# Keys and queries turned in token pairs, growth products written over alpha, and a new order of steps, in a gated-attention and hard-swish kernel

## The chip, the core and the metric

The kernel runs on one core of one Trainium2 chip. The core has five engines with queues of their own: TensorE (PE in the profile; its weight loads are PEld), VectorE (DVE), ScalarE (ACT), GpSimd (POOL), and SyncE (SP), which issues the DMAs. The metric is the device time of one execution in microseconds (us), lower is better. The kernel before takes 533.33 us, the median of three runs from 532.68 to 533.54 us.

## The reference, cut to what matters

```python
def _attn_ref(q, k, v, alpha):            # (4, 8, 768, 48) each
    state = np.zeros((B, H, D, D))
    for t in range(S):
        state = alpha[:, :, t, :, None] * state + np.einsum('bhd,bhe->bhde', k[:, :, t], v[:, :, t])
        y[:, :, t] = np.einsum('bhd,bhde->bhe', q[:, :, t], state)

def _moe_ref(x, w_in, w_out):             # x: attention's output as (3072, 384); d_ff = 2048
    h = x @ w_in
    g = h * np.clip(h + 3.0, 0.0, 6.0) / 6.0
    return g @ w_out
```

A linear attention with a decay for every channel and token is followed by a two-layer network with a hard-swish between the layers. The two weight matrices arrive as 64-bit floats and are rounded to 32 bits on the core.

## The kernel before, in words

**Attention.** The 4 x 768 tokens are cut into 24 chunks of 128. For a chunk `j`, alpha, keys and queries are turned so that a partition holds a channel (two heads of 64 rows each at a time, four such pairs of heads side by side) and the 128 tokens lie along the free dimension. A reversed scan over alpha gives the products R towards the end of the chunk (`decay`, step `r`, L309) and a reciprocal of its four first values goes into the tile `ini` (L313). A forward scan over alpha that starts from `ini` gives the growth products P (`growth`, step `p`, L320). The keys are multiplied by R and the queries by P (`scaled`, steps `k` and `q`, L332). Then come scores (`sc`, L346), mask (`m`, L356), the placing of queries and state beside them (`qa` L366, `sv` L419), the state's update (`u` L430, `sm` L438 and L440, `st` L409) and the attention's output, which is written turned (`ya` and `yb`, L456; `cy`, L465). P and the two `ini` tiles hold 4 x 129 values in a partition: each group of 128 tokens has one value ahead of it, where alpha is 0 so that the scan starts anew.

**How a chunk is turned.** Chunks 0 to 5 are turned by TensorE (steps `ta`, `tk`, `tq`, L282). From chunk 6 (`FIRST = 6`) VectorE turns blocks of 32 x 32 (`by_blocks`, L286). The load (L262) puts token 4u+v of a chunk into block v, row u, so one turn of 128 x 512 reads runs of 32 words and writes each turned row with a step of 4 words:

```python
nc.vector.transpose(out=to.rearrange("r p (u v) -> r p v u", v=V),
                    in_=quads[name, j % NQ][:, :, :, 0:BLK])
```

For keys and queries it writes straight into `Ks[j % 2]` or `Qs[j % 2]`, and `scaled` then multiplies in place. From chunk 8, the scaled keys are turned back by token in another way: a turn on VectorE that writes whole runs (`kt`, L391), a DMA out (`kw`) and a DMA back (`kr`).

**The two layers.** Two chunks make a pair `g` of 256 tokens. Pairs 0 and 1 go through the first layer plainly (steps `f`, `fa`, `fb`, L479 and L490; their gate is `fr` on ScalarE, L495, and `fg` on VectorE, L499), and pair 0 through the second (`b`, L517). Pairs 2 to 11 take the first layer as 20 products of sums of x and sums of weights (`M`, L603), with the sums of weights built once (`y`, L540 to L544), sums of x for every pair (`xc`), copies out of PSUM (`n`, L609), sums of products (`o`), gate (`e` L495, `h` L499). Pairs 1 to 11 take the second layer as 7 products of sums (`P`, L706; sums `s`, L650 and L667; `K`, `G` and `O` bring results out). One `M` step is 8 entries on PE, one `P` step 16.

**The order.** All steps stand in one string of 1798 words, such as `tq.9` or `M.3.10`, under a manual schedule. Each engine runs its own part of that string strictly in order, and waits where data or a buffer is not ready. The last numbers of a word name a PSUM bank: four banks (`t0` to `t3`) serve the attention, four (`m0` to `m3`) the layers. `z` steps are idle matmuls on TensorE that compute nothing. The weights' way is load (`w`), low half (`d1`, L186), magnitude (`d2`, L196), high bits (`d3`, L207 to L210) and addition (`d4`, L217 on GpSimd). In L210 the 64-bit words are worked on in place, so one input and the output step by 2 words.

Of the kernel before, what the change touches and what calls it, by code (L numbers as in the profile page):

```python
# [8 lines left out]
FP = mybir.dt.float32  # L9
# [8 lines left out]
def kernel(  # L18
# [255 lines left out]
    def transposed(name, j, i=None):  # L274
        if j >= FIRST:
            t = (K_t if name == "k" else Q_t)[j] = (Ks if name == "k" else Qs)[j % 2]
            by_blocks(t, name, j)
            return
        t = bank("t" + name, j, i)
        src = ring[name, j % NR]  # L280
        for p in range(NP):
            nc.tensor.transpose(  # L282
                t[:, p], src[:, 2 * p : 2 * p + 2].rearrange("s h d -> s (h d)"), ident)

    def by_blocks(to, name, j):
        nc.vector.transpose(out=to.rearrange("r p (u v) -> r p v u", v=V),  # L286
                            in_=quads[name, j % NQ][:, :, :, 0:BLK])

# [5 lines left out]
    def without_first(t):  # L294
        return t[:, 0 : NP * W].rearrange("r (p w) -> r p w", w=W)[:, :, 1:W]
# [8 lines left out]
    def decay(j):  # L304

        n = NP * W
        ax, ic = aX[j % 2], ini[j % 2]
# [5 lines left out]
        nc.vector.reciprocal(out=ic.rearrange("r (p w) -> r p w", w=W)[:, :, 0:1],  # L313
                             in_=R_t[j][:, :, 0:1])

    def growth(j):

        n = NP * W
        P_t[j] = Ps
        nc.vector.tensor_tensor_scan(  # L320
            out=P_t[j], data0=aX[j % 2][:, 0:n], data1=ini[j % 2], initial=0.0,
            op0=ALU.mult, op1=ALU.add)

    def scaled(name, j):

        if j < FIRST:
# [5 lines left out]
        nc.vector.tensor_tensor(out=t, in0=src, in1=by, op=ALU.mult)  # L332
        (K_t if name == "k" else Q_t)[j] = t
# [423 lines left out]
    with tc.manual_schedule():  # L757
# [18 lines left out]
               p.5 fg.1.3 d2.12 k.5 fg.1.0 d3.12 d4.10 fr.1.6.1 sm.4.1 tq.5.1 sv.4.1 lk.6 w.13  # L776
               fr.1.2.0 d1.11 f.1.4.2 d2.11 d4.12 fg.1.6 q.5 d3.11 p.6 d2.13 la.7 fr.1.4.1 fg.1.4
               f.1.5.0 lv.5.0 qa.4.1 fg.1.2 kb.5.3 fr.1.5.1 w.15 d4.11 d2.15 ca.7 ya.4.1 qa.5.1 tk.6
               yb.4 sc.5.2.0 b.1.0.2 lk.7 k.6 d3.13 d3.15 st.5 ck.5 fa.4.3 m.5 b.1.1 lq.6 w.14 tq.6
               fb.4 fg.1.5 d1.13 d1.15 d4.15 q.6 b.0.0.1 d2.14 fr.0.4.0 d3.14 y.5 d4.13 cy.4 fg.0.4  # L780
               d1.14 d4.14 x.0 y.1 y.10 b.0.1 y.0 y.2 u.5.2 P.1.0.0 K.1.0 qa.5.0 sv.5.0 qa.6.1
               P.1.1.3 b.0.2 b.1.2 kb.6.0 ya.5.3 y.6 s.1.0.0 sm.5.0 sv.5.1 G.1.0.0 tk.7 s.1.1.1
               s.1.2.3 x.1 yb.5 cy.5 b.1.3 sc.6.1.2 lv.6.2 ck.6 u.6.3.0 s.1.3.2 x.2 P.1.2 b.0.3
               K.1.1 y.7 s.1.4 s.1.5 y.11 y.3 r.7 xc.2.1 x.3 y.4 y.8 xc.2.3 k.7 xc.2.0 xc.2.4 y.9
               y.12 y.16 y.13 y.15 P.1.3.3 K.1.2 P.1.4 bo.1 P.1.5 xc.2.5 G.1.1.1 P.1.6 y.14 y.17
               la.8 xc.2.2 xc.2.6 y.19 G.1.3.3 so.1 y.20 G.1.2.2 y.18 M.2.0.2 bo.0 y.21 M.2.15.3
               y.23 sm.6.0 n.2.0.8 z.1.3 M.2.1 M.2.16 xc.2.8 n.2.1.9 xc.2.7 M.2.2 kb.7.3 p.7 lk.8
               O.1.2 lq.7 xc.2.10 sm.6.1 n.2.2.10 ca.8 m.6 M.2.7.0 lq.8 n.2.7.11 M.2.3 M.2.4 M.2.8
               xc.2.9 lv.7.0 r.8 n.2.4.12 tk.8 ck.7 lv.12.1 k.8 M.2.18.1 sv.6.1 o.2.0.0 st.7 M.2.5
               tq.7 kt.8 kw.8 n.2.5.13 M.2.9 q.7 o.2.1.0 sv.6.0 lq.9 o.2.4.0 u.7.1.3 sc.7.1.3 sm.7.0  # L790
               sv.7.0 O.1.3 M.2.10 ya.6.2 yb.6 e.2.1.1 la.9 h.2.1 e.2.0.0 y.22 lv.8.2 p.8 n.2.10.14
               qa.7.0 M.2.11 sv.7.1 M.2.6.2 n.2.18.10 M.2.19 h.2.0 n.2.11.15 qa.7.1 m.7 O.1.1 M.2.12
               cy.6 o.2.6.0 o.2.5.0 ya.7.1 yb.7 n.2.12.12 kr.8 xc.3.2 y.24 M.2.13 lv.9.0 o.2.3.0
               n.2.13.12 cy.7 tq.8 lq.10 sm.7.1 o.2.3.1 M.2.17 o.2.2.0 e.2.3.0 M.2.14 o.2.2.1 xc.3.1
               xc.3.3 la.10 e.2.2.1 P.2.0.1 xc.3.4 xc.3.5 lk.10 xc.3.6 M.3.0.2 q.8 u.8.1.0 lk.9
               sc.8.2.3 n.3.0.12 M.3.1 h.2.2 e.2.5.1 h.2.3 xc.3.0 xc.3.7 o.2.6.1 e.2.6.0 M.3.7.0
               n.3.1.9 o.2.7.0 o.2.7.1 K.2.0.3 h.2.6 M.3.2 P.2.1 qa.8.0 n.3.7.13 e.2.4.0 n.3.2.10
               xc.3.10 xc.3.8 st.8 h.2.5 ca.9 M.3.3 O.1.0 qa.8.1 h.2.4 r.9 s.2.0.14 G.2.0.1 e.2.7.0
# [24 lines left out]
               lq.13 s.4.2.9 P.4.1 h.4.7 xc.5.8 G.4.0.3 s.4.1.12 p.13 M.5.2 tq.13 n.5.2.15 P.4.3.3
               k.13 M.5.3 M.5.4 lq.14 s.4.3.10 K.4.2 sm.12.0 kt.13 n.5.7.8 sm.12.1 O.3.2 s.4.5
# [116 lines left out]
```

## Time and profile before

| | us |
|---|---:|
| median of three runs (532.68 to 533.54) | 533.33 |
| the profiled execution's own time | 533.63 |
| its span, first to last instruction | 531.8 |
| PE busy | 524.3 |
| PEld busy | 494.0 |
| DVE busy | 475.6 |
| ACT busy | 261.4 |
| POOL busy | 50.3 |
| first `M` step starts on PE | 125.65 |
| granted TensorE clock | 1.0 in every slice |

The profiled execution took 533.63 us, of which 531.8 lie between the first and the last instruction and 1.8 around them. It is 0.3 us above the median. PE's records are pipelined and overlap, so a stop of less than about 0.1 us does not show as idle time; it shows only in the distance between the starts of two steps. In the chain that ended last, PE has 85% of the span, VectorE 7% and ScalarE 4%; the `P` products alone have 36% and the `M` products 31%.

### The profile page before, as it was taken

To read this page: it belongs to the slowest core of one execution; us is meant where nothing else is said; L and a number is where in the kernel's file an instruction comes from. 1 tells how busy PE (TensorE), PEld (TensorE's weight loads), DVE (VectorE), ACT (ScalarE), POOL (GpSimd) and SP (SyncE) were. 2 spreads that over 40 slices of the span, in tenths; PEclk is the share of its full clock that TensorE was granted. 3 is DMA by queue.
4 is the path that set the end of the run, shared out by engine and by line. 5 is a ranking of instruction groups with operands and counts; after the bars stand their busy time and mean duration, and the time that the engine had idled before them with its cause. 6 is when DMAs were issued, how large, how long until landed. Compare 5 with 4: busy or idle time off the path is not lost.

```text
span 531.8 us, 15076 instructions
## 1 busy us (share of the span) xinstructions
PE 524.3 (99%) x6290; PEld 494.0 (93%) x6290; DVE 475.6 (89%) x839; ACT 261.4 (49%) x513; POOL 50.3 (9%) x71
## 2 busy tenths in 40 slices
PE   8999999999999999999999999999999999999997
PEld 5798886789999999999999999999999999999997
DVE  7999999999999999999999999998999999486471
ACT  4888875212664453542673554544454454443330
POOL 5333353100000100000000000000000000000000
PEclk9999999999999999999999999999999999999999
DMA  9999867005363253453463553443531532010000
GB/s 177 246 241 251 247 153 177 2 2 133 74 150 84 64 118 77 115 123 89 95 156 85 120 136 91 96 107 69 145 78 20 129 98 48 1 33 7 9 17 30
DMA packets 124100, 54.40 MB, mean 102 GB/s; under 512 B 83328, under 2 KB 116864, under 8 KB 124032
## 3 DMA queue, kind: packets, MB, share of 16 engines
q1 hardware_dynamic: 124032, 53.44, 42.2%
q8 instruction: 49, 0.80, 0.7%
q14 instruction: 19, 0.16, 0.1%
HBM read 44.50 MB, written 8.91 MB: 100 GB/s over the span
## 4 chain that ended last, share of the span: by engine, by line
PE 85%; DVE 7%; ACT 4%; DMA 1%; issue 1%; SPq 1%; POOL 0%; DVEq 0%; ACTq 0%
PE m_ps L706 36%; PE m_ps L603 31%; PE m_ps L479 4%; PE m_ps L517 4%; PE t_ps L456 4%; PE t_ps L346 2%; PE t_ps L430 2%; DMA rings<-in_q_dram 1%; DVE A L356 1%; ACT A L366 1%; DVE g_sb L540 1%; ACT r L495 1%; ACT raw L186 1%; DVE g_sb L499 1%; SPq L251 1%
## 5 line engine op out<-in xcount | busy, mean ns | idle before, releaser
L706 PE MATMUL m_ps<-w,g_sb 128*128 128x192 f32 x704 | 121.7, 326 | 0.0
L609 ACT COPY g_sb<-m_ps 128x512 f32<-128x512 f32 x110 | 63.5, 584 | 104.2 <-PE m_ps L603 86.4
L706 PEld LDWEIGHTS m_ps<-w,g_sb 128*128 128x128 f32 x704 | 113.7, 190 | 0.6 <-DVE g_sb L667 0.3
L706 PE MATMUL m_ps<-rings,g_sb 128*128 128x192 f32 x528 | 91.7, 327 | 0.2 <-DVE g_sb L650 0.2
L706 PEld LDWEIGHTS m_ps<-rings,g_sb 128*128 128x128 f32 x528 | 85.3, 190 | 0.6 <-DVE g_sb L650 0.5
L603 PE MATMUL m_ps<-xc,w 128*128 128x128 f32 x640 | 83.5, 277 | 0.0
L603 PEld LDWEIGHTS m_ps<-xc,w 128*128 128x128 f32 x640 | 77.9, 192 | 1.1
L495 ACT ACTIVATE r<-g_sb,half 128x512 f32<-128x512 f32 x80 | 57.0, 722 | 29.8 <-DVE g_sb L499 11.9
L499 DVE SCALAR_TENSOR_TENSOR g_sb<-r,g_sb 128x512 f32<-128x512 f32 x80 | 53.5, 682 | 8.7 <-ACT r L495 8.4
L603 PE MATMUL m_ps<-xT,raw 128*128 128x128 f32 x400 | 52.8, 277 | 0.0
L603 PEld LDWEIGHTS m_ps<-xT,raw 128*128 128x128 f32 x400 | 48.8, 192 | 0.5 <-ACT g_sb L609 0.2
L409 POOL TENSOR_TENSOR st<-sm,R 128x192 f32<-128x192 f32 x20 | 12.6, 630 | 358.2 <-DVE sm L440 300.5
L650 DVE TENSOR_TENSOR g_sb<-g_sb 128x512 f32<-128x512 f32 (+1 forms) x55 | 42.1, 792 | 3.7 <-PE m_ps L706 3.5
L603 PE MATMUL m_ps<-xT,w 128*128 128x128 f32 x320 | 42.0, 277 | 0.0
L603 PEld LDWEIGHTS m_ps<-xT,w 128*128 128x128 f32 x320 | 39.0, 192 | 0.4
L366 ACT COPY A<-q 48x256 f32<-48x256 f32 x88 | 35.4, 403 | 7.3 <-DVE q L332 6.1
L356 DVE TENSOR_TENSOR A<-t_ps,mask 64x256 f32<-64x256 f32 x96 | 36.2, 416 | 1.2 <-PE t_ps L346 0.8
L479 PE MATMUL m_ps<-xT,w 128*128 128x256 f32 x144 | 33.3, 384 | 0.5 <-POOL w L217 0.3
L603 PE MATMUL m_ps<-xc,raw 128*128 128x128 f32 x240 | 32.1, 277 | 0.1
L479 PEld LDWEIGHTS m_ps<-xT,w 128*128 128x128 f32 x144 | 26.5, 190 | 5.3 <-POOL w L217 0.9
L540 DVE TENSOR_TENSOR g_sb<-g_sb 128x512 f32<-128x512 f32 x40 | 27.2, 682 | 4.6 <-ACT g_sb L609 4.6
L309 DVE TENSOR_TENSOR_SCAN R<-t,ones 128x516 f32<-128x516 f32 x24 | 29.6, 1233 | 1.6 <-ACT t L300 1.6
(105 smaller groups left out, 726.9 us busy)
## 6 DMA issues: line engine op xcount, KB each, us to landing
raw<-in_moe_w_out_dram SPq DMA_DIRECT2D x8, 768.0 KB, 5.5
raw<-in_moe_w_in_dram SPq DMA_DIRECT2D x6, 768.0 KB, 7.3
v<-in_v_dram SPq DMA_DIRECT2D x48, 96.0 KB, 3.1
out_dram<-oh SPq DMA_DIRECT2D x44, 96.0 KB, 1.8
far<-kq SPq DMA_DIRECT2D x64, 64.0 KB, 2.2
kb<-far SPq DMA_DIRECT2D x64, 64.0 KB, 2.0
aq<-in_alpha_dram SPq DMA_DIRECT2D x36, 96.0 KB, 2.5
kq<-in_k_dram SPq DMA_DIRECT2D x36, 96.0 KB, 2.5
```

Source lines behind the costliest of these rows:

```text
L309: nc.vector.tensor_tensor_scan(out=reverse(R, n - 1, n), data0=reverse(ax, n, n), data1=reverse(ones, n, n), initial=0.0, op0=ALU.mult, op ...
L356: nc.vector.tensor_tensor(out=to[:, a], in0=sc[a][half], in1=mask[half, half].unsqueeze(1).to_broadcast([HB, NP, HB]), op=ALU.mult)
L366: nc.scalar.copy(out=to[:, a], in_=Q_t[j][64 * a : 64 * a + D, :, half])
L456: nc.tensor.matmul(y_of(j, (i + 1) // 2, p)[:, HB * b : HB * b + HB], vb[:, p, e : e + 32], A_t[j][:, b, 2 * p + a], start=(b == 0 and i = ...
L479: nc.tensor.matmul(h[:, f], w1[:, kk, o : o + C], xT_t[g][:, kk], start=(kk == 0), stop=(kk == KT - 1))
L495: nc.scalar.activation(out=to, in_=h, func=AF.Relu, bias=half, scale=1.0 / 6.0)
L499: nc.vector.scalar_tensor_tensor(out=to, in0=r, scalar=1.0, in1=h, op0=ALU.min, op1=ALU.mult)
L540: eng.tensor_tensor(out=out, in0=in0, in1=in1, op=ALU.add if s1 > 0 else ALU.subtract)
L603: nc.tensor.matmul(acc[g][i][:, f * C : (f + 1) * C], spots[w][:, f * C : (f + 1) * C], x_of(g, x), start=(first and f == 0), stop=last, s ...
L609: nc.scalar.copy(out=slots[z], in_=acc[g][i])
L650: nc.vector.tensor_tensor(out=out, in0=in0, in1=in1, op=ALU.subtract)
L706: nc.tensor.matmul(to[g], a, rhs[:, f], start=(first and f == 0), stop=(last and f == HF - 1), skip_group_check=True)
```

## The change

1. **Token pairs.** For chunks 6 and later, keys and queries are turned into a place of their own (`places["k"]`, `places["q"]`) in which the two low bits of a token number are split: one bit chooses between two halves of the tile, the other stays beside its neighbour. The turn now writes with a step of 2 words, and `scaled` reads runs of 2 words, from one half and from the other by turns, and writes `Ks` or `Qs` in the order of tokens. Alpha is turned as before.
2. **Growth products over alpha.** For chunks 6 and later the forward scan writes over alpha's own tile. After the queries are multiplied, GpSimd sets the four values ahead of the groups back to 0 (18 new memsets of 128 x 4). For chunks 0 to 5 the products go into the queries' place. One `ini` tile is left of two, with one memset of 128 x 516 fewer at the start.
3. **Order.** From the 203rd word on, the string of steps is another one. It holds the same 1798 steps; 52 of them (scores, updates, first halves of the attention's output, three turns back of keys by token and two turns on TensorE) name other PSUM banks.

```diff
-    aX, ini = [], []
+    aX = []
...
-        t = consts.tile([C, NP * W], FP, tag=f"ini{r}")
-        nc.vector.memset(t, 0.0)
-        ini.append(t)
+    ini = consts.tile([C, NP * W], FP, tag="ini")
+    nc.vector.memset(ini, 0.0)
...
-    Ps = consts.tile([C, NP * W], FP, tag="P", name="P")
+    places = {name: consts.tile([C, NP * W], FP, tag=f"{name}t", name=f"{name}t")
+              for name in "kq"}
+    turns = {name: t[:, 0 : NP * C].rearrange("r (w p n) -> r w p n", w=2, p=NP)
+             for name, t in places.items()}
...
         if j >= FIRST:
-            t = (K_t if name == "k" else Q_t)[j] = (Ks if name == "k" else Qs)[j % 2]
-            by_blocks(t, name, j)
+            turned(name, name, j)
             return
...
+    def turned(to, name, j):
+        nc.vector.transpose(
+            out=turns[to].rearrange("r w p (u b) -> r p w b u", b=V // 2),
+            in_=quads[name, j % NQ].rearrange("r p (w b) d -> r p w b d", w=2)[..., 0:BLK])
+
+    def in_pairs(to):
+        return turns[to].rearrange("r w p (u b) -> r p u w b", b=V // 2)
+
+    def pairs(x):
+        return x.rearrange("r p (u w b) -> r p u w b", w=2, b=V // 2)
...
     def growth(j):
-        P_t[j] = Ps
-        nc.vector.tensor_tensor_scan(
-            out=P_t[j], data0=aX[j % 2][:, 0:n], data1=ini[j % 2], initial=0.0,
-            op0=ALU.mult, op1=ALU.add)
+        P_t[j] = places["q"] if j < FIRST else aX[j % 2]
+        to = P_t[j][:, 0:n]
+        nc.vector.tensor_tensor_scan(out=to, data0=aX[j % 2][:, 0:n], data1=ini, initial=0.0,
+                                     op0=ALU.mult, op1=ALU.add)

     def scaled(name, j):
+        t = (K_t if name == "k" else Q_t)[j] = (Ks if name == "k" else Qs)[j % 2]
+        by = R_t[j][:, :, 1:W] if name == "k" else without_first(P_t.pop(j))
         if j < FIRST:
-            src = ps_t.pop(("t" + name, j))
-            t = (Ks if name == "k" else Qs)[j % 2]
-        else:
-            src = t = (K_t if name == "k" else Q_t)[j]
-        by = R_t[j][:, :, 1:W] if name == "k" else without_first(P_t.pop(j))
-        nc.vector.tensor_tensor(out=t, in0=src, in1=by, op=ALU.mult)
-        (K_t if name == "k" else Q_t)[j] = t
+            nc.vector.tensor_tensor(out=t, in0=ps_t.pop(("t" + name, j)), in1=by, op=ALU.mult)
+            return
+        nc.vector.tensor_tensor(
+            out=pairs(t), in0=in_pairs(name), in1=pairs(by), op=ALU.mult)
+        if name == "q":
+            first = aX[j % 2][:, 0 : NP * W].rearrange("r (p w) -> r p w", w=W)[:, :, 0:1]
+            nc.gpsimd.memset(first, 0.0)
...
-               d2.8 cy.3 d3.8 fr.0.6.1 w.9 ca.6 w.4 fr.0.7.0 fg.0.7 lv.4.1 ck.4 d2.9 d3.9 f.1.1.1
-               q.4 st.4 d1.9 fr.1.1.0 fg.1.1 sv.4.0 f.1.0.2 ca.5 sc.4.1.0 u.4.1.0 fg.0.6 r.5 d1.4
-               f.1.7.0 r.6 f.1.3.3 d4.8 d2.4 w.10 tk.5.3 d4.9 w.11 dx.4 fr.1.7.1 sm.4.0 d3.4 w.12
-               d2.10 qa.4.0 fg.1.7 fr.1.3.1 m.4 lq.5 d1.10 f.1.6.0 d3.10 d1.12 d4.4 fr.1.0.0 f.1.2.1
...
+               d2.8 cy.3 d3.8 ck.4 lq.5 tk.5.1 fr.0.6.1 d4.8 fg.0.6 fr.0.7.0 w.9 d2.9 q.4 w.4 tq.5.3
+               fg.0.7 ca.5 f.1.1.1 lv.4.1 w.10 d2.4 st.4 d1.4 d1.9 ca.6 f.1.0.2 la.7 r.5 f.1.7.0
+               fr.1.1.0 dx.4 d1.10 fr.1.7.1 d3.9 p.5 fg.1.1 d2.10 lv.5.0 d3.4 d4.9 fr.1.0.0 w.11
+               f.1.3.3 w.12 fg.1.7 k.5 qa.4.0 d2.11 f.1.2.1 r.6 kb.5.1 ck.5 lq.6 d3.10 f.1.6.0 q.5
...
+               q.14 e.5.0.0 ca.16 M.5.19 M.5.10 P.4.4 sv.12.1 m.13 n.5.10.10 G.4.2.0 sm.13.0 lq.15
...
```

More of the change, by code (lines that the diff above doesn't have):

```diff
@@ L306, in decay @@
         n = NP * W
-        ax, ic = aX[j % 2], ini[j % 2]
+        ax = aX[j % 2]
         R = Rs[j % 2]
@@ L312, in decay @@
         R_t[j] = R.rearrange("r (p w) -> r p w", w=W)
-        nc.vector.reciprocal(out=ic.rearrange("r (p w) -> r p w", w=W)[:, :, 0:1],
+        nc.vector.reciprocal(out=ini.rearrange("r (p w) -> r p w", w=W)[:, :, 0:1],
                              in_=R_t[j][:, :, 0:1])
@@ L776 @@
[L776 to L798, printed above, removed]
@@ new lines @@
+               y.9 b.1.3 y.2 y.10 lk.8 s.1.5 y.15 P.1.3.3 y.11 cy.4 y.4 k.7 xc.2.1 xc.2.3 K.1.2
+               P.1.4 xc.2.4 y.13 x.3 bo.1 P.1.5 y.16 xc.2.5 G.1.1.1 qa.6.1 sm.6.0 y.17 sv.6.0 y.19
+               so.1 y.12 G.1.2.2 y.20 tk.8 bo.0 y.18 xc.2.0 P.1.6 y.21 G.1.3.3 la.8 xc.2.10 M.2.0.2
+               y.23 lv.7.0 kb.7.2 xc.2.6 lq.7 xc.2.8 n.2.0.8 M.2.15.3 ck.7 M.2.1 xc.2.2 n.2.1.9
+               M.2.16 M.2.2 z.1.3 xc.2.7 n.2.2.10 M.2.7.0 p.7 lq.8 M.2.3 n.2.7.11 ca.8 r.8 M.2.4
+               M.2.8 n.2.4.12 xc.2.9 sm.6.1 st.7 y.14 O.1.1 k.8 m.6 M.2.18.1 o.2.0.0 sv.6.1 tq.7
@@ new lines @@
+               M.2.5 M.2.9 kt.8 e.2.0.0 q.7 o.2.1.0 kw.8 h.2.0 sv.7.0 sc.7.0.3 u.7.0.1 e.2.1.1
+               sm.7.0 n.2.5.13 M.2.10 lv.12.1 y.22 lq.9 n.2.10.14 h.2.1 ya.6.2 yb.6 O.1.2 lk.9
+               M.2.11 p.8 cy.6 y.24 n.2.18.10 M.2.6.2 n.2.11.15 M.2.12 sv.7.1 kr.8 m.7 o.2.4.0
+               xc.3.2 sm.7.1 lv.8.2 n.2.12.12 M.2.19 o.2.3.0 M.2.17 qa.7.0 qa.7.1 o.2.5.0 M.2.13
+               O.1.3 n.2.13.12 ya.7.1 yb.7 o.2.3.1 tq.8 la.9 cy.7 o.2.2.0 o.2.6.0 xc.3.1 lk.10
+               xc.3.3 o.2.2.1 M.2.14 xc.3.0 e.2.3.0 xc.3.4 xc.3.5 P.2.0.1 M.3.0.2 e.2.2.1 q.8
@@ new lines @@
+               M.4.15.1 o.4.3.1 n.4.13.14 o.4.2.0 M.4.16 ya.10.3 yb.10 sv.11.1 o.4.4.0 o.4.7.0
+               o.4.2.1 lq.14 cy.10 O.3.1 r.13 ya.11.1 yb.11 kw.12 e.4.2.1 M.4.14 cy.11 k.13 sv.12.0
+               xc.5.1 e.4.3.0 xc.5.3 lv.13.2 kr.12 M.4.19 o.4.5.0 P.4.0.2 xc.5.4 xc.5.5 xc.5.0
+               M.5.0.0 o.4.6.0 M.4.17 n.5.0.14 h.4.3 o.4.6.1 xc.5.7 xc.5.2 e.4.4.0 O.3.2 xc.5.6
+               h.4.2 K.4.0.3 e.4.6.1 xc.5.8 p.13 h.4.4 u.12.1.3 sc.12.1.0 h.4.6 xc.5.9 q.13 kt.13
+               M.5.1 o.4.7.1 lk.14 e.4.5.0 la.16 P.4.1 n.5.1.13 s.4.0.11 la.15 G.4.0.3 h.4.5 e.4.7.1
@@ new lines @@
+               xc.7.0 P.6.0.1 tk.18 G.5.3.0 xc.7.5 xc.7.2 h.6.3 xc.7.6 K.6.0.0 kr.17 o.6.6.1 M.7.0.2
+               h.6.2 e.6.6.1 o.6.7.1 O.5.3 P.6.1 n.7.0.14 e.6.7.0 xc.7.7 M.7.1 M.7.7.3 ca.18
+               n.7.7.13 u.16.3.0 r.18 u.17.1 h.6.6 n.7.1.10 xc.7.8 xc.7.10 sc.17.3.2 sc.16.1.0
+               sv.16.0 h.6.7 s.6.0.8 s.6.2.12 s.6.1.9 G.6.0.0 sm.16.0 k.18 M.7.2 n.7.2.11 lk.19
+               sm.16.1 M.7.8 M.7.3 M.7.4 n.7.4.15 qa.16.1 m.16 qa.17.0 p.18 qa.18.0 P.6.3.0 o.7.0.0
+               tk.19 M.7.9 sv.16.1 st.17 qa.17.1 M.7.5 s.6.3.8 K.6.2 s.6.5 e.7.0.0 kt.18 xc.7.9
@@ new lines @@
+               n.7.5.9 m.17 o.7.1.0 P.6.2 M.7.18.2 sv.17.0 lq.19 e.7.1.1 s.6.4 h.7.1 n.7.18.8
+               o.7.6.0 ca.19 M.7.10 M.7.19 n.7.10.12 sm.17.0 h.7.0 M.7.11 n.7.11.15 K.6.1 o.7.5.0
+               P.6.5 e.7.5.0 kw.18 sv.17.1 tq.18 G.6.2.1 q.18 M.7.12 n.7.12.11 o.7.7.0 P.6.4 h.7.5
+               M.7.13 n.7.13.8 M.7.6.0 kr.18 ya.16.2 yb.16 cy.16 ya.17.1 G.6.1.2 yb.17 u.18.0.2
+               cy.17 xc.8.1 M.7.14 o.7.2.0 o.7.6.1 O.6.2 xc.8.3 M.7.15.2 xc.8.4 sm.18.0 O.6.1
+               o.7.3.0 o.7.3.1 M.7.16 o.7.2.1 e.7.2.0 xc.8.5 xc.8.0 P.6.6 so.0 G.6.3.1 xc.8.6 la.20
@@ new lines @@
+               o.7.4.0 xc.8.7 lv.19.0 M.8.0.3 xc.8.10 r.19 M.7.17 O.6.3 M.8.7.1 n.8.0.11 M.8.1
+               sm.18.1 e.7.6.1 h.7.2 h.7.6 n.8.7.8 o.7.7.1 e.7.7.0 xc.8.8 P.7.0.0 xc.8.2 h.7.7
+               e.7.3.1 n.8.1.12 lk.20 k.19 kt.19 h.7.3 tk.20 lq.20 K.7.0.2 qa.18.1 p.19 kw.19
+               e.7.4.1 h.7.4 ca.20 sc.18.0.1 kr.19 st.19 M.8.2 s.7.0.14 P.7.1 s.7.1.10 M.8.8 n.8.2.9
+               G.7.0.2 r.20 M.8.3 O.7.0 la.21 sv.18.1 M.8.4 s.7.2.13 lk.21 n.8.4.15 o.8.0.0 P.7.3.2
+               tq.19 M.8.9 k.20 lv.20.1 s.7.3.14 m.18 o.8.1.0 kt.20 kw.20 e.8.1.0 P.7.2 M.8.10 q.19
@@ new lines @@
+               s.8.3.14 M.9.5 n.9.5.12 m.20 p.22 P.8.2 sm.20.1 st.21 lq.23 o.9.1.0 s.8.5 M.9.18.0
+               K.8.2 qa.20.0 M.9.10 e.9.1.1 K.8.1 O.7.3 n.9.10.10 P.8.5 G.8.2.2 ca.23 lk.23 k.22
+               M.9.11 sc.21.2.1 u.21.2.1 O.8.2 M.9.15.3 qa.21.1 n.9.18.14 h.9.1 n.9.11.11 M.9.12
+               M.9.19 M.9.16 P.8.4 sm.21.0 kt.22 o.9.6.0 n.9.12.8 o.9.7.0 sv.21.0 M.9.13 o.9.5.0
+               o.9.4.0 m.21 e.9.4.1 sv.21.1 r.23 M.9.17 G.8.1.0 kw.22 o.9.3.0 n.9.13.8 M.9.6.0
+               o.9.3.1 e.9.3.0 ya.21.0 ya.20.3 yb.20 yb.21 lv.23.2 M.9.14 o.9.7.1 h.9.3 tk.23 cy.21
@@ new lines @@
+               qa.22.1 O.8.3 u.23.3 u.22.1.2 sc.23.1.2 sm.22.0 sv.22.1 sm.22.1 s.9.5 sv.22.0 qa.22.0
+               qa.23.0 sc.22.3.0 m.22 M.10.10 P.9.4 st.23 sm.23.0 n.10.10.12 M.10.11 n.10.11.10
+               e.10.1.0 e.10.0.1 M.10.5 h.10.0 P.9.5 qa.23.1 n.10.5.15 G.9.1.1 M.10.12 P.9.6
+               n.10.12.13 o.10.3.0 M.10.13 sv.23.1 xc.10.9 G.9.3.2 G.9.2.3 m.23 M.10.15.0 M.10.6.1
+               n.10.13.13 M.10.18.3 h.10.1 M.10.16 o.10.2.0 O.9.3 n.10.18.13 o.10.7.0 o.10.2.1
+               o.10.3.1 sv.23.0 ya.22.3 yb.22 ya.23.2 yb.23 cy.22 cy.23 e.10.3.1 o.10.6.0 o.10.4.0
@@ new lines @@
+               O.9.1 xc.11.1 M.10.14 M.10.19 o.10.6.1 e.10.2.0 o.10.5.0 h.10.2 xc.11.3 M.10.17
+               e.10.5.0 xc.11.4 O.9.2 xc.11.5 P.10.0.2 K.10.0.3 M.11.0.1 h.10.5 xc.11.6 h.10.3
+               e.10.6.1 o.10.7.1 e.10.4.0 xc.11.0 xc.11.7 n.11.0.13 P.10.1 xc.11.2 h.10.4 xc.11.8
+               e.10.7.0 M.11.1 h.10.7 h.10.6 s.10.1.14 n.11.1.10 G.10.0.2 M.11.7.0 s.10.0.15
+               s.10.2.12 O.9.0 M.11.2 P.10.3.3 xc.11.10 O.10.0 n.11.2.11 xc.11.9 M.11.3 s.10.3.8
+               s.10.4 n.11.7.9 s.10.5 M.11.8 M.11.4 P.10.2 n.11.4.14 o.11.0.0 K.10.1 M.11.9 M.11.5
@@ new lines @@
+               K.10.2 P.10.5 o.11.1.0 M.11.10 e.11.0.0 n.11.5.15 G.10.2.0 M.11.18.3 e.11.1.1
+               M.11.15.1 n.11.10.8 h.11.0 M.11.11 M.11.16 h.11.1 n.11.18.14 n.11.11.12 o.11.4.0
+               M.11.19 o.11.7.0 e.11.4.1 O.10.2 M.11.12 o.11.5.0 P.10.4 n.11.12.11 M.11.13 M.11.17
+               o.11.6.0 o.11.3.0 n.11.13.14 h.11.4 o.11.7.1 G.10.1.1 M.11.6.3 O.10.1 M.11.14
+               o.11.3.1 P.10.6 o.11.6.1 e.11.5.0 o.11.2.0 o.11.2.1 e.11.6.1 h.11.6 e.11.7.1 h.11.5
+               s.11.0.11 G.10.3.0 h.11.7 e.11.2.0 s.11.1.8 s.11.2.14 s.11.3.9 P.11.0.1 K.11.0.0
```

182 lines of the change are left out of this document (72 added, 110 removed).

## The prediction, made before the changed kernel ran

> **What bounds the kernel now.** I read the page first, then the busy time in stretches, then single steps on TensorE, then the chain of waits. The page's first part lists each engine's busy time, its share of the span and its instructions:
>
> ```profile
> PE 524.3 (99%) x6290; PEld 494.0 (93%) x6290; DVE 475.6 (89%) x839; ACT 261.4 (49%) x513; POOL 50.3 (9%) x71
> ```
>
> TensorE is full. VectorE's 89% is a mean over two halves, as the stretches of 20 us show. Columns: stretch, its length, then busy time of PE, PEld, DVE, ACT and POOL, then the granted clock, the DMA share and GB/s.
>
> ```profile
> 160.00:180.00 20.00, 20.00 (x206) 19.72 (x206) 19.84 (x35) 8.28 (x19) 0.90 (x1) 1.00 0.29 70
> 400.00:420.00 20.00, 19.82 (x141) 19.52 (x140) 19.73 (x32) 9.66 (x23) 0.52 (x1) 1.00 0.32 69
> 480.00:500.00 20.00, 20.00 (x157) 20.00 (x156) 9.48 (x16) 6.90 (x14) 0.00 (x0) 1.00 0.03 11
> ```
>
> From 20 to 440 us VectorE has 18 to 20 us of work in every 20, so both engines run at their limit; behind that it has room. How much TensorE loses is read from the starts of its steps in the timeline (start, length, engine, line):
>
> ```profile
> 397.26 0.57 PE L430 MATMUL t_ps<-v,kb 64*48 64x48 f32 x32
> 397.65 0.66 PE L346 MATMUL t_ps<-q,k 48*64 48x64 f32 x32
> 398.24 1.16 PE L603 MATMUL m_ps<-xc,w 128*128 128x128 f32 x8
> 399.24 1.06 PE L603 MATMUL m_ps<-xT,raw 128*128 128x128 f32 x8
> 400.13 2.77 PE L706 MATMUL m_ps<-w,g_sb 128*128 128x192 f32 x16
> ```
>
> A clean `M` step takes 0.89 us from start to start (399.24 to 400.13), a clean `P` step 2.60. The `M` step behind the small matmuls takes 1.00 (398.24 to 399.24), and the one ahead of them 0.99 (396.27 to 397.26): each crossing between small and full matmuls costs 0.1 us. Taken step by step like this, TensorE's stops from the first `M` step (125.65 us) on sum to only 2.1 us; between 54.7 us, where the new order begins to differ on PE, and 125.65 to 1.9 us. The largest late one is 0.45 us. The chain of waits names its cause (start, length, what held the chain):
>
> ```profile
> 405.51 1.18 DVE k L286
> 406.70 0.52 DVE k L332
> ...
> 408.73 1.15 DVE g_sb L650
> ...
> 410.70 0.70 DVE g_sb L650
> 411.40 0.04 issue
> 411.44 1.57 PE m_ps L706 x8
> ```
>
> A turn of keys, 1.18 us long, delays VectorE's sums, and `P` waits for them. Turns of queries stand in the chain at 135.69 and 146.59 us as well, the second ahead of 0.1 us lost at 151.17.
>
> **The change, part by part.** The costs are mean times of one instruction, from the groups by shape (busy, mean ns):
>
> ```profile
> L286 DVE STREAM_TRANSPOSE k<-kq 128x512 f32<-128x512 f32 x18 | 20.1, 1116 | 0.5 <-PE t_ps L346 0.4
> L332 DVE TENSOR_TENSOR k<-k,R 128x512 f32<-128x512 f32 x18 | 12.3, 685 | 0.1
> L391 DVE STREAM_TRANSPOSE kq<-k 128x512 f32<-128x512 f32 x16 | 11.2, 698 | 0.1
> L210 DVE SCALAR_TENSOR_TENSOR raw<-raw,w 128x768 uint32<-128x768 uint32 x11 | 10.6, 960 | 0.4
> ```
>
> *Turns.* 36 turns (18 of keys, 18 of queries) now write with a step of 2 words. The trace has the turn with a step of 4 words, 1117 ns, and the one that writes whole runs, 698. A shorter one than the second is excluded: no pattern is simpler than whole runs. L210 reads and writes with a step of 2 words; against the dense L332 it takes 275 ns more for 256 more elements, 1.07 ns each, which also makes L332's 512 elements: it pays nothing for the step. So I take 698: 36 x 0.42 = 15.1 us less VectorE work; bounds 0 to -15.1.
>
> [...]
>
> *Multiplications.* The 36 products now read pairs of words from two places 1 KB apart. No row shows that. Lower bound 685 ns as now, since the dense form is no slower than any other; upper bound 685 + 420, the most that a scattered pattern costs a 512-element row here. I take 685, because two neighbours are read at a time as L210's step also stays within few words; for the range, 0 to +15.1 us.
>
> *Growth over alpha.* The scan (L320, 1267 ns) keeps its length and its place on VectorE's queue: 0. The 18 memsets on GpSimd lie between its 128x1 memset of 0.11 us and its 128x128 one of 0.21: at most 3.8 us on an engine that is 9% busy. They are a new wait, though: alpha's next turn into that tile waits on VectorE for GpSimd, and all of VectorE's queue stands behind it. In the new order 14 of the 16 gaps between the queries' product and that turn hold 3 us or more of other VectorE work; only `q.14`, `ca.16` and `q.19`, `ca.21` follow at once. Between 0.1 and 0.6 us each (the latter if a state's update of 0.63 us stands ahead on GpSimd); VectorE then has more saved than that, so I take 0 for the end, up to +1.0. The `ini` memset that goes (0.49 us at the start) lies beside transfers that land later, at 3.9 us: 0.
>
> *Order.* The work on TensorE is the same. Counted in the two orders, its crossings between small and full matmuls fall from 78 to 68: 10 x 0.1 = -1.0 us. The end, from 470 us on, has the same order on TensorE. Loads move too: SP now issues chunk 5's queries behind the first alpha of chunk 6, ahead of two weight slices of 768 KB; in the trace that place is at 47.4 us and the next load landed at 53.7, and the turn on PE comes near 54: 0 to +0.5, taken as 0.
>
> *Stops.* With prices as I take them, VectorE's work ahead of pair 6's first `P` is 295.9 us instead of 300.2 (each row's mean less the 0.055 us by which records overlap, added in each order). So the late stops that VectorE causes should shrink: of 2.1 us I take 1.3 away, bounds 0 and 2.1. For the early 1.9 us I take no change (bounds -1.3 and +4.4, the latter from the last rival): only four turned rows fall ahead of the first `M` step, and the order there is simply another.
>
> Sum: -1.0 - 1.3 = -2.3 us. On the profiled execution's own 533.63 this gives 531.3, on the median, 0.3 lower, **531.0 us**. What is late next is TensorE's own work, so 15 us off VectorE buy only this.
>
> **The rivals.** A difference within 0.2% (1.07 us) can't be told from none.
>
> *New stops take the place of the old.* For it: the order is other throughout, and 2 us of stops in 400 are few for any order. Against: VectorE is lighter from chunk 6 on. Then no stop shrinks, and of the crossings' 1.0 us the two waits for GpSimd and the later load take back up to 0.7: 533.33 - 1.0 + 0.7 = 533.0.
>
> [...]
>
> *One early bottleneck.* The new order puts five `f` steps of pair 1 in a row on TensorE, 12.9 us, with four banks; the fifth waits for `fg.1.1`. Before, VectorE had one product (0.68 us) between `f.1.1` and `fg.1.1`; now it has a turn, a decay, the high bits of a slice and a growth: 1.12 + 1.41 + 2.20 + 1.27 = 6.0 us. TensorE's cover is four steps of 2.58, 10.3 us; it breaks when VectorE is over 3.6 us behind there. In the profile such a wait for `fg` cost 0.4 us at 72 us. If each of two slices' high bits comes out in full, 2 x 2.2 us: 535.4.
>
> **How the numbers follow.** Forecast 531.0 with chance 0.56 (its own range 529.3 to 532.4), stops replaced 0.15, VectorE no lighter 0.14, early bottleneck 0.15. Faster by over 0.2% needs less than 532.26: nearly all of the forecast and a little of the second case, 0.57; within 0.2%: 0.15; slower: 0.28. The low end is all stops shrunk by more, -1.0 - 2.1 - 1.3 of the early ones: 528.9. The high end takes in the two slower cases but for their worst fifth: 536.8.
>
> **What would show it.** Right: turns of keys and queries near 700 ns, products near 685, VectorE busy near 460 us, `M` and `P` at 0.89 and 2.60 us, TensorE's stops behind the first `M` step near 0.8 us, and that step still near 125.6 us. Wrong: products at 0.9 us or more, the first `M` step over 127 us (the early case), or stops of over 2 us behind it that start at a turn of alpha which waits for GpSimd.

## The result: 540.11 us, slower, and the profile after

The changed kernel takes 540.11 us (median of four runs, 537.99 to 540.66) against 533.42 us for the kernel before on the same chip: a ratio of 1.0121, 95% interval 1.0092 to 1.015. The profiled execution of the changed kernel is its quickest run, 537.99 us with a span of 536.2; the other three have spans of 538.3 to 538.9.

The page's first part, as before: busy us, share of the span, instructions.

```profile
PE 525.3 (98%) x6290; PEld 495.3 (92%) x6290; DVE 465.9 (87%) x838; ACT 261.3 (49%) x513; POOL 50.3 (9%) x89
```

VectorE is 9.7 us less busy, not the 15 of the turns: taken one by one its instructions last 13.5 us less (decay's scan, for one, rose from 1233 to 1269 ns), and its records overlap by 3.7 us less. TensorE is as full as it was, and the span is 4.4 us longer. The medians lie 6.7 us apart, so this profile shows two thirds of the loss. The groups by shape (busy, mean ns, idle before and its cause) show that every price of the code came out as taken:

```profile
L287 DVE STREAM_TRANSPOSE t<-aq 128x512 f32<-128x512 f32 x18 | 20.0, 1111 | 0.4 <-POOL t L347 0.4
...
L291 DVE STREAM_TRANSPOSE kt<-kq 128x512 f32<-128x512 f32 x18 | 12.7, 703 | 0.0
L343 DVE TENSOR_TENSOR k<-kt,R 128x512 f32<-128x512 f32 x18 | 12.6, 698 | 0.1
L291 DVE STREAM_TRANSPOSE qt<-qq 128x512 f32<-128x512 f32 x18 | 12.5, 695 | 0.0
...
L343 DVE TENSOR_TENSOR q<-qt,t 128x512 f32<-128x512 f32 x18 | 12.2, 678 | 0.1
```

Turns with a step of 2 words take 0.70 us, the products that read pairs 0.69, and alpha's turns wait 0.4 us for GpSimd's memset in the whole run. The stretches (length, busy PE, PEld, DVE, ACT, POOL, clock, DMA share, GB/s) tell where TensorE lost. First one of the kernel before:

```profile
100.00:120.00 20.00, 20.00 (x209) 15.25 (x208) 19.97 (x31) 2.69 (x7) 0.00 (x0) 1.00 0.02 7
```

and those of the changed kernel:

```profile
100.00:120.00 20.00, 18.03 (x266) 15.08 (x267) 19.86 (x30) 2.92 (x8) 0.64 (x3) 1.00 0.01 2
160.00:180.00 20.00, 19.72 (x143) 19.19 (x141) 19.75 (x34) 8.77 (x20) 0.62 (x2) 1.00 0.34 78
340.00:360.00 20.00, 20.00 (x293) 19.73 (x293) 13.47 (x29) 6.97 (x14) 0.90 (x2) 1.00 0.31 82
```

TensorE loses 2 us between 100 and 120, where it lost nothing before, 0.9 from 120 to 140, and tenths in later stretches such as that from 160 to 180. VectorE's saving shows as idle time elsewhere: 6.5 us from 340 to 360 us, where nothing waits for it. The starts of TensorE's steps in the timeline have the prices of before:

```profile
229.85 1.16 PE L617 MATMUL m_ps<-xc,w 128*128 128x128 f32 x8
230.85 1.06 PE L617 MATMUL m_ps<-xT,w 128*128 128x128 f32 x8
231.74 2.77 PE L720 MATMUL m_ps<-w,g_sb 128*128 128x192 f32 x16
234.72 1.16 PE L617 MATMUL m_ps<-xc,raw 128*128 128x128 f32 x8 [0.21 <-DVE xc L556]
```

A clean `M` step is 0.89 us (230.85 to 231.74), one behind small matmuls 1.00; the `P` step at 231.74 should take 2.60 and took 2.98, because the next `M` waited for a sum of x.

The two profiles compare in three parts. TensorE's orders part at 54.72 us before and already at 53.89 us in the changed kernel, though all its steps ahead of that point are the same. The other runs reach it at 53.8 to 55.1 us, so these 0.8 us are scatter. From there to the first `M` step, which came at 126.38 in place of 125.65 us, TensorE took 72.48 in place of 70.93 us: +1.55, with 6 crossings of 0.1 us fewer, so the stops on this way grew by 2.15 us. Behind it, a count of all losses against clean steps and 0.1 us a crossing, the smallest ones too (the prediction's count was coarser), grew from 2.93 to 6.99 us, with 4 crossings fewer: +4.07 - 0.4 = +3.67, and the stretch to the end took 409.84 in place of 406.17 us. The chain of waits reaches back only to 460 us and names one stop of this size.

**The first large stop.** The timeline of the changed kernel has it on three engines (start, length, engine, line; in brackets the idle time before and what ended it). VectorE:

```profile
89.67 0.96 DVE L209 SCALAR_TENSOR_TENSOR raw<-raw,w 128x768 uint32<-128x768 uint32 x1
...
96.04 0.68 DVE L343 TENSOR_TENSOR q<-qt,t 128x512 f32<-128x512 f32 x1
98.38 1.94 DVE L556 TENSOR_TENSOR raw<-w 128x512 f32<-128x512 f32 x1 [1.65 <-POOL w L216]
```

GpSimd:

```profile
96.79 0.11 POOL L347 MEMSET t<- 128x4 f32 x1 [8.91 <-DVE q L343]
96.88 2.89 POOL L216 TENSOR_TENSOR w<-raw 128x768 int32<-128x768 int32 x2
```

TensorE:

```profile
109.85 1.57 PE L720 MATMUL m_ps<-rings,g_sb 128*128 128x192 f32 x8 [1.54 <-DVE rings L664]
```

The high bits of weight slice 15 are ready at 90.6 us. Its addition `d4.15` stands in GpSimd's queue behind the new memset, which waits for `q.6` until 96.8 us. VectorE, full from 100 to 140 us (19.86 and 19.82 us of each 20), waits 1.65 us for the weights, and TensorE 1.54 us for what VectorE makes of them. VectorE's sum at 98.38 us also takes 1.94 us, where such sums took 0.68 in the kernel before (the group's mean); GpSimd's additions run beside it until 99.77. In e4 below it is the next sum, at 97.25 us, that stands beside an addition, and that one takes 1.95 us. Why is not tested.

### The profile page after: what moved, and what is told of

Same layout as the page of the kernel before. It is cut to its first block, busy times and chain, and to the rows that moved or that the text cites. A ratio compares the mean times of both kernels' runs of the same rounds, so it can differ in the third digit from the quotient of the medians.

```text
span 536.2 us, 15106 instructions
## 1 busy us (share of the span) xinstructions
PE 525.3 (98%) x6290; PEld 495.3 (92%) x6290; DVE 465.9 (87%) x838; ACT 261.3 (49%) x513; POOL 50.3 (9%) x89
## 5 line engine op out<-in xcount | busy, mean ns | idle before, releaser
L321 DVE TENSOR_TENSOR_SCAN R<-t,ones 128x516 f32<-128x516 f32 x24 | 30.5, 1269 | 2.9 <-ACT t L312 2.7
L617 PEld LDWEIGHTS m_ps<-xc,raw 128*128 128x128 f32 x240 | 29.9, 192 | 1.4 <-DVE g_sb L558 0.5
```

Source lines behind the costliest of these rows:

```text
L321: nc.vector.tensor_tensor_scan(out=reverse(R, n - 1, n), data0=reverse(ax, n, n), data1=reverse(ones, n, n), initial=0.0, op0=ALU.mult, op ...
L617: nc.tensor.matmul(acc[g][i][:, f * C : (f + 1) * C], spots[w][:, f * C : (f + 1) * C], x_of(g, x), start=(first and f == 0), stop=last, s ...
```

## The experiments

Theories: **(A)** the new order loses the time through TensorE's waits for single steps; **(B)** the new memset's place in GpSimd's queue loses it. Times are medians in us; ratios are to the kernel before on the same chip (533.27 to 533.45 us).

| kernel | us | ratio, 95% interval |
|---|---:|---|
| changed kernel | 540.11 | 1.0121, 1.0092 to 1.015 |
| new code, old order, first splice (e2) | 535.71 | 1.004, 1.0027 to 1.0054 |
| old code, new order (e3) | 547.01 | 1.0257, 1.0231 to 1.0282 |
| memset on VectorE (e1) | 539.71 | 1.0116, 1.0093 to 1.014 |
| `d4.15` ahead of `q.6` (e4) | 538.05 | 1.008, 1.0063 to 1.0096 |
| new code, old order, second splice (e5) | 534.96 | 1.0028, 1.0018 to 1.0039 |
| old start, new rest (h1) | 539.29 | 1.0107, 1.0091 to 1.0123 |
| new start, old rest (h2) | 533.26 | 0.9996, 0.9986 to 1.0006 |
| the same, memset on VectorE (h2v) | 532.43 | 0.9987, 0.9975 to 0.9999 |
| new code, old order, third splice (e6) | 532.58 | 0.9984, 0.9975 to 0.9992 |
| five steps moved (e7) | 538.04 | 1.0089, 1.0076 to 1.0101 |
| new order to pair 5, old rest (h3) | 536.28 | 1.0053, 1.004 to 1.0067 |
| three places moved (e9) | 535.29 | 1.0043, 1.0029 to 1.0056 |
| e9 to pair 5, old rest (h4) | 535.38 | 1.0041, 1.0028 to 1.0055 |
| loads of chunk 8 earlier (e10) | 538.03 | 1.0083, 1.0068 to 1.0099 |

### Code and order apart: e2, e3, e5, e6

e2, e5 and e6 have the new code under the order of before. Its single places for turns and `ini` ask for a few moved words: `p.17` right ahead of `r.18`, `tk.22` behind `k.21`, and `r.6` and `p.5` the other way round, which the three do differently.

```diff
 the words of before, in order: r.5 d1.4 f.1.7.0 r.6 ... p.5 fg.1.3 ... q.5 d3.11 p.6
 e2
-f.1.7.0 r.6 ... p.5 fg.1.3
+f.1.7.0 ... p.5 r.6 fg.1.3
 e5
-f.1.7.0 r.6 ... q.5 d3.11 p.6
+f.1.7.0 ... q.5 d3.11 r.6 p.6
 e6
-f.1.7.0 r.6 ... p.5 fg.1.3
+f.1.7.0 p.5 r.6 ... fg.1.3
```

> The code of the changed kernel under the order of the kernel before; three steps of that order are moved a little (r.6 behind p.5, p.17 ahead of r.18, the turn tk.22 behind k.21), because the changed code has one place for each turn. If the order loses the time (theory A), the cheaper turns show as in the forecast: VectorE about 10 to 14 us less busy than before, 531 to 533 us, ratio to before 0.995 to 1.000. If the code loses it (GpSimd's new memset, single places for turns, waits that these make: theory B), 536 to 540 us.

> The changed code under the order of before once more, with the decay r.6 put right ahead of the growth p.6, where no gate of the first product chain waits behind it (in the run before, r.6 behind p.5 held a gate back and cost 3 us at 71 us, and from the first M step on that run was 0.85 us shorter than before). If the cheaper steps of VectorE are worth what that run showed behind the first M step, 531.5 to 533 us, ratio 0.997 to 0.999. If the changed code itself delays something early (rival), 534 us or more, with the first M step behind 127 us again.

> The changed code under the order of before, now with growth p.5 moved ahead of decay r.6 (r.6 where it stood), so that both are done before the last gates of the first product chain. In the two runs before, a decay put in late held up a gate, PE stood for 2.0 to 2.2 us and the granted clock fell to 0.66 to 0.79 for the next 5 to 8 us. If those stops were the whole loss of the changed code in the old order, the first M step comes at 125 to 126 us, 405.4 us follow, and the time is 532 to 533 us, ratio 0.997 to 0.999. If the code costs something of its own early, 534 us or more.

e2 lies just under theory B's numbers and e5 where its rival had it, but for a reason of the splice: the moved decay held a gate back, TensorE stood for 2.18 and 1.96 us, and the first `M` step came at 128.7 and 128.0 us. e6 has no such stop, its first `M` step at 124.9 us, and 532.58 us. So the new code alone is worth 0.16%, 0.85 us (by its interval 0.4 to 1.3), in the old order.

e3 is the old code under the new order, with the turns `tq.6`, `tk.12`, `tk.18`, `tk.20` and `tk.22` right ahead of their products and `p.17` behind `q.16`.

> The code of the kernel before under the order of the changed kernel; the turns of q of chunk 6 and of k of chunks 12, 18, 20 and 22 stand right ahead of their products and growth 17 behind q.16, because the code of before turns into the places of q and k themselves. No step of GpSimd is new here. If the order loses the time by itself (theory A), 538 to 543 us: the PE stops between 85 and 130 us and those behind the second P step stay, and turns of 1.1 us make them longer. If the memset's place in GpSimd's queue is most of it (theory B), 533 to 536 us.

It took 547.01 us, longer than theory A had it: without a memset on GpSimd, and with dearer turns, the new order is 13.6 us slower than the old. The code made the new order's loss smaller, not larger.

### The memset: e1 and e4

```diff
 e1
-            nc.gpsimd.memset(first, 0.0)
+            nc.vector.memset(first, 0.0)
 e4
-... q.6 b.0.2 d4.15 ...
+... d4.15 q.6 b.0.2 ...
```

> The changed kernel with the first column of alpha cleared by VectorE in place of GpSimd; nothing else moves. If the weight additions d4.15 and d4.14 wait behind that memset on GpSimd (theory B), they run at about 91 and 96 us in place of 96.9 and 98.3, VectorE's 1.65 us wait at 96.7 us is gone, and the span falls by 1 to 2.5 us, to 537.5 to 539 us. If that wait is covered further on and the order loses the time (theory A), 539.5 to 541 us: 18 more instructions of about 0.1 us on VectorE, and nothing back.

> The changed kernel with one step of the order moved: GpSimd's weight addition d4.15 two places earlier, ahead of q.6, whose memset held it back. Theory B: the addition runs at about 91 us, VectorE's wait of 1.65 us is gone, PE's stop of 1.5 us at 108 us shrinks to under 0.5, and the time is 1 to 2.5 us below the changed kernel's 540.1, so 537.5 to 539 us. Theory A: within 0.5 us of 540.1, with the stop elsewhere.

GpSimd's lines of e4, in the timeline:

```profile
90.61 1.47 POOL L216 TENSOR_TENSOR w<-raw 128x768 int32<-128x768 int32 x1 [2.89 <-issue]
96.79 0.11 POOL L347 MEMSET t<- 128x4 f32 x1 [4.71 <-DVE q L343]
```

The addition runs at 90.6 us, VectorE's wait is gone, TensorE's stop of 1.54 us is 0.27, and the median is 2.1 us lower: theory B holds for some 2 us. This holds more firmly for the start than for the whole. From the point where the orders part to the first `M` step, the six profiles with this move and the same words up to there (e4, e7, e9, h2, h3, h4) take 69.2 to 71.5 us, the two without it (the changed kernel and e10) 72.5 and 71.7: 2.2 us between the means. At the end it rests on the medians, of six and of four runs, which lie over 2.7 us in both cases and overlap (536.38 to 539.08 against 537.99 to 540.66). In e4's own profile, a run of 538.32 us, the gain is lost again behind the first `M` step, most of it where the `u` step of chunk 8 waits for its operands (TensorE's lines of e4; in the changed kernel's profile the wait here is 0.22 us):

```profile
153.83 0.26 PE L444 MATMUL t_ps<-v,kb 64*48 64x48 f32 x2 [1.56 <-issue]
154.71 0.53 PE L444 MATMUL t_ps<-v,kb 64*48 64x48 f32 x28 [0.62 <-DMA v<-in_v_dram]
```

e1 moves the first `M` step 3.0 us forward, to 123.39 us, and yet gains 0.4 us: in its profile the stretch from there to the end is 2.8 us longer than the changed kernel's, 1.2 of it at 150 to 154 us, where the `u` step of chunk 8 waits for its load, the rest in other stops grown by tenths. Theory A's number was right there.

### Start and rest apart: h1, h2, h2v, h3

Each takes one order's words up to a cut and then the words that are left in the other's order: h1 the old (with e5's moves) up to `M.2.0`, h2 the new (with e4's move), h3 as h2 with the cut at `M.5.0`, with e6's moves in the old part.

> The changed code; the order of before up to the first M step, then the steps that are left in the order of the changed kernel. From the first M step to the end the changed kernel took 409.8 us, before 406.2. If the loss sits in the rest of the order (theory A), 536.5 to 540 us. If it sits in the start alone (GpSimd's queue and the late weight slices, theory B), 531.5 to 533.5 us.

> The changed code; the order of the changed kernel up to the first M step, with the weight addition d4.15 ahead of q.6, then the steps that are left in the order of before. Theory A (the rest of the order is the loss): first M step at about 124.7 us and 405 to 406.5 us behind it, 531.5 to 533 us. Theory B: the stops between 127 and 180 us come from what the start left behind (loads and VectorE's arrears) and stay, 535 to 539 us.

> As the run before it, and the first column of alpha cleared by VectorE in place of GpSimd (there the first M step came at 123.4 us in an earlier run). Theory A: 530 to 532.5 us, under the kernel before. Theory B: the millisecond fractions won at the start are lost again at 150 us, 535 to 539 us.

> The changed code; the order of the changed kernel (d4.15 ahead of q.6) up to the first M step of group 5 (about 233 us), then the steps that are left in the order of before. With the cut at the first M step of group 2 it took 533.3 us, without a cut 538.05. If the loss of the rest is spread as the stops of the profile are (about 3 us from 127 to 235, 2 us behind that), 536 to 537 us. If it is one early place that everything behind follows from, 538 us; if it is all late, 533.5 us.

(In the third text, fractions of a microsecond are meant.) With the old rest the new start is level with the kernel before (h2), and 1.0 us under it with the memset on VectorE (h2v; its interval overlaps h2's, and by its ratio it is level with e6); with the new rest the old start is at 539.29. With the start held the same, the new rest costs 4.3 us (h1 less e5) and 4.8 us (e4 less h2). Most of the loss sits in the rest: theory A. h3 lies between, but its cut makes a stop of its own, 1.40 us at 240 us, so its 536.28 counts as some 534.9. h1's figure holds e5's stop at 80 us as well. In h2's profile the first `M` step comes 2.2 us sooner than before, and 1.18 us of that are lost at once, at 127 us, in a wait for a sum of weights.

### Which waits: e7, e9, h4, e10

The stops of the new rest in the timelines begin where a short step that TensorE needs stands behind a chunk's long ones on VectorE, or behind loads on SP.

```diff
 e4, and:
-M.2.0.2 y.23 ... xc.2.6                 +M.2.0.2 xc.2.6 y.23          (e7, e9, h4)
-r.10 ... h.3.1 h.3.0                    +h.3.1 h.3.0 r.10             (e7, e9, h4)
-lk.9 ... lv.8.2                         +lv.8.2 lk.9                  (e7)
-lk.9 ... kr.8 ... lv.8.2                +lv.8.2 kr.8 lk.9             (e9, h4; e10 alone, without e4's move)
-r.13 ... k.13 ... xc.5.8                +xc.5.8 r.13 p.13 ... k.13    (e7)
-m.19 ... xc.8.9                         +xc.8.9 m.19                  (e7)
```

> The changed kernel with d4.15 ahead of q.6 (538.05 us in an earlier run) and, in the rest of its order, five places where a PE step waits for a short step that stands behind a chunk's turns, decay or mask on VectorE, or behind loads on SP: xc.2.6 ahead of the sum y.23, the load of v of chunk 8 ahead of lk.9, h.3.1 and h.3.0 ahead of decay r.10, r.13 and k.13 behind xc.5.8, xc.8.9 ahead of mask m.19. If these places are the loss of the rest (theory A), the stops at 129, 153, 179, 234 to 245 and 383 us shrink from 3.4 to 5.4 us together to under 1.5, and the time is 534 to 536 us. If VectorE has too much to do there in any order (rival), the stops come back at the next steps and the time stays at 537 to 538.5 us.

e7 gained nothing over e4, as the rival said, but its profile says why. The losses from 125 to 200 us fell from 5.0 (e4's) to 2.8 us; moving `r.13` behind the sums of x put it with `p.13`, 2.5 us of scans, in front of two gates, and two new stops came up (TensorE's lines of e7):

```profile
239.56 1.16 PE L617 MATMUL m_ps<-xT,raw 128*128 128x128 f32 x8 [0.92 <-ACT g_sb L623]
241.66 1.16 PE L617 MATMUL m_ps<-xc,w 128*128 128x128 f32 x8 [0.94 <-DVE g_sb L556]
```

The `xc.8.9` move changed nothing at 383 us.

> The changed kernel with d4.15 ahead of q.6 and three of the five moves of the run before: xc.2.6 ahead of y.23; h.3.1 and h.3.0 ahead of decay r.10; the load of v of chunk 8, and here the read of k of chunk 8 too, ahead of lk.9. r.13, k.13 and xc.8.9 stand where the changed kernel has them. If single places make the loss (theory A), the two stops of 0.9 us at 239 and 242 us are gone again, those at 129, 153 and 178 us stay small, and the time is 535 to 536.5 us. If VectorE's work is what is short there (rival), 537 to 538.5 us.

> As the run before up to the first M step of group 5, then the steps that are left in the order of before. With the same cut and without the three moves it took 536.28 us; with the old order from group 2 on, 533.3. If the three places are the loss from 127 to 235 us (theory A), 533.5 to 534.8 us; if not, 535.8 us or more.

> The changed kernel with two steps moved, both on SP's queue: the load of v and the read of k of chunk 8 ahead of the load of k of chunk 9. In the profiles the u step of chunk 8 waits at 152 to 156 us for that load, 0.4 to 2.4 us, and where PE stood still for 1.8 us the clock fell to 0.79 to 0.87 behind it. If this wait is part of the loss and of the scatter of the changed kernel's runs (537.6 to 541.8 us), the time is 538 to 539.3 us and the runs lie within 2 us; if it is hidden, 540.1 us.

e9, without those two moves and with `kr.8` moved beside `lv.8`, took 535.29 us, 2.8 below e4: theory A. h4 missed by 0.6 us; its cut makes a stop of 1.40 us at 234 us, so it can't tell more than that. e10 moves SP's words alone, and its median is 2.1 us below the changed kernel's; its runs lie between 536.1 and 538.9, wider than the 2 us expected, and overlap the changed kernel's. The two profiles don't show the gain, for the one of the changed kernel, its quickest run, waits only 0.22 us at this place (537.99 us against 537.66): that its other runs wait there for longer, as e4, e3 and h3 do, is likely but not seen. SP's own waits from 100 to 180 us show what the load stood behind, first in the kernel before, then in the changed one (line, what ended the wait: us in total, times, longest):

```profile
SPq L396 <- DVE q L332: 6.6, 1, 6.6
```

```profile
SPq L410 <- DVE q L343: 10.9, 1, 10.9
```

The write of chunk 8's keys (`kw.8`) waits on SP for their turn on VectorE (L391 before, L405 now; the view names a neighbour of it): SP comes to it sooner and issues it at 139.0 in place of 137.35 us, and the whole queue stands behind it. In the old order `lv.8` follows ahead of `kr.8` and its issue begins at 145.9 us; in the new one it follows the load of k of chunk 9 and `kr.8` and begins at 150.5. TensorE's lines of h3 show the cost when it comes late:

```profile
154.02 0.26 PE L444 MATMUL t_ps<-v,kb 64*48 64x48 f32 x2 [0.86 <-issue]
155.19 0.53 PE L444 MATMUL t_ps<-v,kb 64*48 64x48 f32 x28 [0.92 <-DMA v<-in_v_dram]
...
156.17 3.29 PE L617 MATMUL m_ps<-xc,w 128*128 128x128 f32 x16
```

and those of e10 that it is gone:

```profile
153.74 0.57 PE L444 MATMUL t_ps<-v,kb 64*48 64x48 f32 x32
154.13 0.66 PE L360 MATMUL t_ps<-q,k 48*64 48x64 f32 x32
154.72 2.05 PE L617 MATMUL m_ps<-xc,w 128*128 128x128 f32 x16
```

## Why the prediction was wrong, point by point

The sum as the runs give it: code -0.85 (e6); memset's place +2.1 (e4); loads of chunk 8 +2.1 (e10); `xc.2.6`, `h.3.1` and `h.3.0` +0.7 (e9's 2.8 less e10's 2.1); what is left, 535.29 - 532.58 = +2.7. That is 533.4 + 6.75 = 540.15, where 540.11 was measured. The terms are differences between neighbours, from the kernel before over e6, e9 and e4 to the changed one, so they must add up to it; that they do is no check. Each of the two terms of 2.1 is uncertain by about 1.5 us, an estimate from the scatter of the runs. The +2.7 was not taken apart on the chip; in e9's profile the seven stops of 0.27 to 0.60 us behind 228 us add to 2.66, and e6's has none of that size there. That the effects simply add is itself not tested beyond e9. The new order also names other PSUM banks in 52 steps, and no run changes these alone; in the changed kernel's profile TensorE's waits of 0.2 us or more from 126 us on end with a result of VectorE, a copy by ScalarE or a load, so banks are not excluded where a copy ends them.

- **Turns -15.1 us, products 0: right.** 700 and 688 ns where 698 and 685 were taken. The case "VectorE no lighter", with its chance of 0.14, did not come: a turn of 512 columns that writes with a step of 2 words took 695 to 703 ns, as one that writes whole runs (697). L209's 963 ns (960 before) had pointed the right way, though the prediction's working from it was circular, since two rows always fit some fixed cost and some cost an element. L650's dense rows support it: 687, 1216 and 1752 ns for 512, 1024 and 1536 elements, 1.04 ns an element, put a dense row of 768 at some 950 ns.
- **The memset: wrong step.** The forecast asked who waits for the memset (alpha's turns: 0.4 us, as priced) and not what stands behind it in GpSimd's queue. There the term, 0 with a bound of +1.0, measured some 2 us (2.1 in the medians, 2.2 up to the first `M` step).
- **Crossings -1.0: right.** Ten fewer in the traces, 78 to 68, still 0.1 us each.
- **Loads: wrong place.** 0 to +0.5 was for weight slices behind queries. Those do land later (the last at 92.4 in place of 88.3 us), but at no cost that shows: in h2 it lands at 91.1, and the first `M` step comes at 123.5 us. The costly load was another one, v of chunk 8 behind `kw.8`, 2.1 us by the medians, on a queue that the forecast followed only at 47 us.
- **Late stops -1.3: the step that failed most, with the wrong sign.** It let stops shrink with VectorE's work; measured in the profile they grew by 4.07 us. They depend on which steps stand ahead of the one that TensorE needs. With the old rest the same code takes 406.7 us from the first `M` step to the end (h2's profile), with the new one 409.8. The forecast counted VectorE's work up to a few points and never followed, in the new order, which steps stand ahead of an `xc`, an `h` or a load.
- **Early stops 0:** +2.15 in the profile; with the addition moved ahead of the memset (e4) the stretch up to the first `M` step takes 70.65 us, 1.8 less and 0.3 less than before.
- **The rivals.** "One early bottleneck" did not happen: between 50 and 75 us TensorE lost 0.14 us after, 1.22 before; five `f` steps in a row held. "New stops take the place of the old" was the right case, but was priced as if stops could only stay as large as they were; no case had the late ones grow while VectorE's work shrank. The upper end, 536.8, was built from other cases and lay 3.3 us low; one of them was "VectorE no lighter", and no run shows the dearer turns or products that its 0.14 and its share in that end stand for: the turns took 0.70 us, the products 0.69.
- **The signs.** None of the three signs of being wrong came up: the products took 0.69 us, the first `M` step came at 126.38 us, and alpha's turns waited 0.4 us in all. Of the signs of being right, turns, products and the steps' prices came out, VectorE was busy for 465.9 us in place of some 460, and the stops behind the first `M` step, near 0.8 us in the forecast, were 7.0.

## What to carry to other kernels

When a change puts a new instruction on a side engine or moves a wait on SP, read what is queued behind it and when each of those was ready: a 0.1 us memset cost some 2 us that way. Work taken off a full engine pays only where a step that the bound engine needs comes sooner (the new code, with turns of 0.70 us in place of 1.12, bought 0.85 us in the old order); compare, for every such step, what stands ahead of it in the old order and the new. To test an order, splice it with the old one at a point where the numbered buffers agree, and look for a stop that the splice itself makes.

## What the runs showed of the hardware that was not expected

In e5 a stop of TensorE of 1.96 us cost almost double. Stretches of 1 us behind it (it lasted from 79.2 to 81.2 us; columns as above, the clock is the third number from the end):

```profile
81.00:82.00 1.00, 0.84 (x2) 0.54 (x3) 1.00 (x3) 0.69 (x1) 0.19 (x2) 0.68 0.99 178
82.00:83.00 1.00, 1.00 (x3) 0.49 (x2) 1.00 (x2) 0.84 (x2) 0.00 (x0) 0.50 0.26 56
83.00:84.00 1.00, 1.00 (x3) 0.60 (x2) 0.97 (x3) 0.99 (x4) 0.00 (x0) 0.50 0.81 139
84.00:85.00 1.00, 1.00 (x3) 0.52 (x3) 0.96 (x2) 0.98 (x2) 0.00 (x0) 0.61 0.72 224
85.00:86.00 1.00, 1.00 (x8) 0.74 (x7) 0.97 (x3) 1.00 (x2) 0.00 (x0) 1.00 1.04 400
```

The granted clock was 0.68, 0.50, 0.50 and 0.61 in the four stretches from 81 to 85 us and 1.00 in the next: 0.32 + 0.50 + 0.50 + 0.39 = 1.71 us lost on top of the 1.96, which at one half makes some 3.4 us (an estimate from these rows, 1.71 / 0.50). The same followed stops of 2.18 us (e2: 0.67, 0.50, 0.50 and 0.63 from 75 to 79 us), 1.97 (h1: 0.83 from 79 to 89 us) and two of 0.86 and 0.92 within 2.1 us (h3: 0.87 and 0.79 in the two stretches of 5 us from 153 us; its two `M` steps above took 3.29 us, e10's 2.05) or of 0.98 and 0.83 (e3: 0.70 and 0.96 in those from 155 us). It did not follow 1.54 us (changed kernel: 1.00 from 107 to 114 us), nor 1.56 and 0.62 us within 2.5 us (e4: 1.00 from 150 to 162 us), which add up to more than h3's, so the length of the stop alone does not decide it; what does is not shown. The other runs of e5 point the same way: five of its eight had a mean clock of 0.996 or 0.997 and took 534.86 to 535.75 us, three had 1.000 and took 533.96 to 534.37.

The lower clock is a likely part of the scatter of e1's runs: two of the six, 541.8 and 541.0 us, had mean clocks of 0.997 and 0.996, the other four, at 1.000, took 537.6 to 540.2. The changed kernel's four runs, 538.0 to 540.7 us, all had 1.000, so their scatter has another cause, which stays open.
